# Norms of the output tiles: sums taken with the residual's addition, squares summed on ScalarE, constant and power on GpSimd

## The chip, the cores and the metric

The kernel runs on one core of a Trainium2 chip. The metric is the device time of one execution in microseconds; lower is better. The core has TensorE (PE, with its weight loads PEld), VectorE (DVE), ScalarE (ACT), GpSimd (POOL) and SyncE (SP, which issues the transfers here). Each engine works through its own queue in order; semaphores make one engine wait for another.

## The reference

Four layers over a sequence of 2048 rows of 640 numbers, all in float32: attention, Fourier mixing, attention, Fourier mixing, each on the normalized input and added to it.

```python
def _layernorm(x, axis=-1, eps=1e-5):
    m = jnp.mean(x, axis=axis, keepdims=True)
    v = jnp.var(x, axis=axis, keepdims=True)
    return (x - m) / jnp.sqrt(v + eps)
...
    def _A_ref(x, wqkv, wo):
        B, S, D = x.shape
        H = 32; Dh = D // H; W = 256
        qkv = (x @ wqkv) ...                      # 32 heads of 20
        scores = jnp.einsum("bhqd,bhkd->bhqk", q, k) * (Dh ** -0.5)
        # a query sees itself and the 255 keys before it
        ...
        return o.reshape(B, S, D) @ wo
    def _B_ref(x, dft_seq_re, dft_seq_im, dft_hid_re, dft_hid_im):
        a = jnp.einsum("bsd,ed->bse", x, dft_hid_re)
        b = jnp.einsum("bsd,ed->bse", x, dft_hid_im)
        return jnp.einsum("ts,bse->bte", dft_seq_re, a) - jnp.einsum("ts,bse->bte", dft_seq_im, b)
    x = x + _A_ref(_layernorm(x), wqkv, wo)
    x = x + _B_ref(_layernorm(x), ...)
    x = x + _A_ref(_layernorm(x), wqkv, wo)
    x = x + _B_ref(_layernorm(x), ...)
```

## The kernel before

The 2048 rows are 16 tiles (NB) of 128 rows (P), each 640 (D) columns wide. Every product is made of three matmuls: each operand is split into a high part, which is its rounded copy, and a low part, the difference, and high x high, high x low and low x high are summed (`product3`, L172). `split` makes the parts: ScalarE copies the high part (L159), VectorE or GpSimd subtracts for the low one (L165).

An attention layer ends with its output product. The product of a tile is summed in two steps: three of five chunks of the attention output are multiplied early (`partials`, added to the residual at L900, so that `y_part(t)` holds the input plus a part of the output), and the last two in `late`. There, for each tile t, 12 matmuls (two halves of 320 columns, two chunks, three matmuls) go to banks 5 and 6 in turn, and VectorE adds bank and `y_part(t)` into the new tile `xw` (L993), which is the layer's result and is stored. In the same place the next layer's norm begins: `stats` takes mean and variance of `xw` on VectorE (two statistics, L217, one aggregation, L219, the constant, L221), a further small operation gives minus the mean (L999), GpSimd raises variance plus constant to the power -1/2 (`root`, L1004), and `norm` lets ScalarE write (xw - mean) * inverse over `y_part(t)`: a small one for the bias (L957) and a large one (L954). The normalized tile is then cut into high and low parts for the Fourier layer (`split_x`: ScalarE's high part at L159, GpSimd's low part at L165). Tiles 8 and up are first added to tile t-8 in their last 256 columns by GpSimd (`sum1`, L1070), and GpSimd takes a difference for a later product (`sum3`, L1074).

The Fourier layer's first product runs along the sequence and starts while the output tiles still come. Its steps are units (`unit`, `seq`), of 9 matmuls each (L1292): a1 0 to a1 7 take tiles 0 to 7, a2 j takes tiles j and j+8. A unit is emitted behind a tile once the parts it needs have been emitted (`need`, `normed`). Each unit also cuts the sequence matrix for the next units (`cut_to`: VectorE's differences at L1198, high parts at L159, low parts at L165).

The order of work is written out by the program. `post(delay, fn)` puts a step `delay` slots later; `tick` goes on by one slot and emits the steps that are due, in the order in which they were posted. After the heads, `spend` counts 0.147 us for each matmul of a tile and 2.05 us for a unit, and ticks once for each 0.65 us (PACE). Here `root` is posted 2 slots behind its tile, `sum3` 4, `norm` and the store of the tile 5; `norm` posts the cut into parts 2 slots later for tiles below 8, and for the others `sum1` 1 and the cut 3 slots later. The last two tiles (t14, t15, called `fast`) have the root at once and are normalized by VectorE in part (`norm_last`, L969). The waits are put in by the framework wherever one engine needs what another wrote.

Of the kernel before, what the change touches and what calls it, by code (L numbers as in the profile page):

```python
# [7 lines left out]
F32 = mybir.dt.float32  # L8
# [3 lines left out]
AF = mybir.ActivationFunctionType  # L12
OP = mybir.AluOpType
# [4 lines left out]
P = 128  # L18
S = 2048
D = 640  # L20
# [5 lines left out]
NB = S // P  # L26
# [3 lines left out]
EPS = 1e-5  # L30
# [33 lines left out]
class Net:  # L64
# [883 lines left out]
    def late(self, xsrc, xdst, hook):  # L948
        nc = self.nc
        ks = range(EARLY, KC)  # L950
        w = dict(zip(ks, self.late_w))

        def scaled(t, xw, st, nm, c0, c1):
            nc.scalar.activation(self.y_part(t)[:, c0:c1], xw[:, c0:c1], AF.Identity, bias=nm[:, 1:2], scale=st[1][:, 1:2])  # L954

        def norm(t, xw, st, nm):
            nc.scalar.activation(nm[:, 1:2], nm[:, 0:1], AF.Copy, scale=st[1][:, 1:2])  # L957
            scaled(t, xw, st, nm, 0, D)
            if t < NB // 2:
                self.post(2, lambda: self.split_x(t, 0, 384))  # L960
            else:
                j = t - NB // 2
                self.post(1, lambda: self.sum1(j, nc.gpsimd))
                self.post(3, lambda: self.split_x(j, 384, 640))

        def norm_last(t, xw, st):

            xn, j = self.y_part(t), t - NB // 2
            nc.vector.tensor_scalar(out=xn[:, 384:], in0=xw[:, 384:], scalar1=st[0][:, 0:1], scalar2=st[1][:, 1:2],  # L969
                                    op0=OP.subtract, op1=OP.mult)  # L970
            self.sum1(j, nc.vector)
            self.post(1, lambda: self.split_x(j, 384, 640, nc.vector))

        def norm_rest(t, xw, st, nm):
            nc.scalar.activation(nm[:, 1:2], nm[:, 0:1], AF.Copy, scale=st[1][:, 1:2])
            scaled(t, xw, st, nm, 0, 384)

        for t in range(NB):
            sb, i = t // 4, t % 4
            y = self.y_part(t)  # L980
            xw = self.raw()
            both = [slice(hf * 320, (hf + 1) * 320) for hf in range(2)]
            if not self.after:
                ps = [self.bank("w", 320) for _ in both]
                yield from self.in_turn(ps, [self.out_terms(self.late_o[sb], w, ks, i, hf) for hf in range(2)])
                for p, cs in zip(ps, both):
                    nc.vector.tensor_tensor(out=xw[:, cs], in0=p, in1=y[:, cs], op=OP.add)
            else:
                for hf, cs in enumerate(both):
                    p = self.bank("o", 320)  # L990
                    for _ in self.product3(p, self.out_terms(self.late_o[sb], w, ks, i, hf)):
                        yield 1
                    nc.vector.tensor_tensor(out=xw[:, cs], in0=p, in1=y[:, cs], op=OP.add)  # L993
                    if hf == 0:
                        yield 1
            self.post(5, lambda t=t, xw=xw: nc.sync.dma_start(xdst[t * P:(t + 1) * P, :], xw))
            st = self.stats(xw, False)
            nm = self.ln.tile([P, 2], F32, name="nb", tag="nb")
            nc.vector.tensor_scalar_mul(nm[:, 0:1], st[0][:, 0:1], -1.0)  # L999
            self.let_go()  # L1000
            fast = t >= NB - 2

            def root(st=st):
                nc.gpsimd.tensor_tensor(out=st[1][:, 1:2], in0=st[1][:, 0:1], in1=self.half, op=OP.pow)  # L1004
            if fast:
                root()
            else:
                self.post(2, root)
            if NB // 2 - 1 <= t < NB - 1:
                self.post(4, lambda t=t: self.sum3(t - NB // 2 + 1))  # L1010
            if fast:
                d = 3 if t == NB - 2 else 0
                self.post(4 + d, lambda t=t, xw=xw, st=st: norm_last(t, xw, st))
                self.post(8 + d, lambda t=t, xw=xw, st=st, nm=nm: norm_rest(t, xw, st, nm))
            else:
                self.post(5, lambda t=t, xw=xw, st=st, nm=nm: norm(t, xw, st, nm))
            if t == NB - 2:
                u = self.last_a2 - 1
                self.post(3, lambda u=u: self.staged(u, 0, nc.vector))
                self.post(6, lambda u=u: self.staged(u, 1))  # L1020
                self.post(9, lambda u=u: self.staged(u, 2))
            hook(t)
            self.late_t = t + 1
            yield 0
# [728 lines left out]
```

## Time and profile before

| | |
|---|---|
| time, median of 3 runs | 2170.54 us (2169.17 to 2170.84) |
| profiled execution, its own time | 2169.7 us |
| its span, first to last instruction | 2168.0 us |
| granted TensorE clock | 0.998 |
| busy: TensorE, VectorE, ScalarE, GpSimd | 98%, 74%, 54%, 43% |
| the tiles' additions, L993 | 64 times, 478 ns median, 523 to 1662 us |
| the statistics of all norms, L217 | 128 times, 475 to 480 ns median by form |
| the tiles' powers, L1004 | 32 times, 552 ns median, 1007 ns at most |
| the tiles' normalization, L954 (640 columns) | 28 times, 923 ns mean |

The profiled execution is one run of the program; its time is the span plus some 1.7 us around it. A row in order of time gives start and length in us, the engine, the line, the operation, output <- inputs with their shapes, how many alike follow each other, and in brackets how long the engine stood idle before it and which instruction ended that. A row of a group gives busy time in us and the mean length of one in ns, then idle time. In the chain of waits each piece is what the next one waited for. The two attention layers have the same sequence of work; the second runs 1078 us later than the first.

### The profile page before, as it was taken

What the parts mean: (1) busy time and instruction counts of PE and PEld (TensorE: products, weight loads), DVE (VectorE), ACT (ScalarE), POOL (GpSimd) and SP (SyncE); (2) the same over time, 40 slices, a digit from 0 to 9 for tenths busy, and PEclk for the clock granted to TensorE, in tenths of its full rate; (3) what the DMA queues carried; (4) which work ended last, traced back from release to release, by engine and by line L of the source; (5) the groups of instructions that cost most, each with busy time, mean ns of one, the idle gap of its engine ahead of it and who ended that gap; (6) DMA issues with size and microseconds to landing.
All of it is one profiled execution on the core that took longest, in us unless ns stands there. A gap on an engine that the chain in (4) does not pass through costs nothing.

```text
span 2168.0 us, 49263 instructions
## 1 busy us (share of the span) xinstructions
PE 2114.2 (98%) x17893; PEld 1765.7 (81%) x17893; DVE 1613.7 (74%) x3936; ACT 1167.3 (54%) x2611; POOL 923.4 (43%) x1455
## 2 busy tenths in 40 slices
PE   7999999899999999999999999998999999999999
PEld 7987777687878888889999877776777788888899
DVE  6448888786897868787751578887778868687787
ACT  2218877766554545543431288786765545455522
POOL 2037776876423234230230477777754323242300
PEclk9999999999999999999999999999999999999999
DMA  5556666786435453657646466667864454546653
GB/s 193 164 168 194 200 196 206 221 228 195 143 123 179 133 181 127 230 197 254 213 145 185 151 202 187 208 194 230 227 185 136 124 189 137 165 152 215 224 175 125
DMA packets 221619, 395.41 MB, mean 182 GB/s; under 512 B 39360, under 2 KB 85952, under 8 KB 221376
## 3 DMA queue, kind: packets, MB, share of 16 engines
q1 hardware_dynamic: 221376, 392.26, 57.0%
q8 instruction: 141, 2.31, 0.5%
q14 instruction: 102, 0.84, 0.1%
HBM read 273.94 MB, written 117.05 MB: 180 GB/s over the span
## 4 chain that ended last, share of the span: by engine, by line
PE 84%; DVE 5%; POOL 4%; ACT 4%; DMA 2%; issue 1%; SPq 0%; ACTq 0%; DVEq 0%; POOLq 0%
PE banks L1292 29%; PE banks L172 15%; PE banks L190 14%; PE banks L636 8%; PE banks L1547 6%; PE banks L606 6%; PE banks L576 4%; POOL big L165 1%; ACT big L954 1%; PE banks L272 1%; DVE qp L165 1%; POOL ou L1222 1%; PE banks L588 1%; POOL rs L1004 1%; ACT big L159 1%
## 5 line engine op out<-in xcount | busy, mean ns | idle before, releaser
L581 DVE CUSTOM_DVE_ANT_0 banks<-banks,mask 128x384 f32<-128x384 f32 (+2 forms) x1024 | 525.4, 559 | 153.5 <-PE banks L576 116.1
L615 ACT ACTIVATE pt<-banks 128x384 f32<-128x384 f32 (+2 forms) x1024 | 430.1, 472 | 139.9 <-PE banks L576 65.8
L606 PE MATMUL banks<-qp,kp 61*128 61x384 f32 (+2 forms) x1024 | 302.7, 365 | 10.1 <-DMA qp<-mt 7.8
L621 POOL TENSOR_SCALAR_AFFINE_SELECT pt<-pt 128x256 f32<-128x256 f32 x512 | 210.1, 411 | 178.1 <-ACT pt L615 130.2
L576 PE MATMUL banks<-kp,qp 60*128 60x384 f32 (+2 forms) x1024 | 279.3, 359 | 4.8 <-DVE mc L581 4.5
L190 PE MATMUL banks<-big,wc 64*128 64x512 f32 x1920 | 272.2, 394 | 0.4 <-DVE pt L394 0.4
L606 PEld LDWEIGHTS banks<-qp,kp 61*128 61x128 f32 x1024 | 176.9, 185 | 68.1 <-issue 27.3
L636 PE MATMUL banks<-pt,vq 128*32 128x128 f32 x5760 | 214.8, 277 | 4.1 <-POOL pt L621 4.0
L190 PEld LDWEIGHTS banks<-big,wc 64*128 64x128 f32 x1920 | 182.8, 185 | 29.6 <-ACT x L500 6.7
L636 PEld LDWEIGHTS banks<-pt,vq 128*32 128x32 f32 x5760 | 143.9, 109 | 64.7 <-issue 48.0
L576 PEld LDWEIGHTS banks<-kp,qp 60*128 60x128 f32 x1024 | 163.7, 185 | 27.4 <-DVE mc L581 16.4
L1222 POOL TENSOR_TENSOR pt<-pt,pt 128x512 f32<-128x512 f32 x36 | 62.3, 1730 | 290.4 <-DMA pt<-c 206.7
L625 POOL TENSOR_SCALAR_AFFINE_SELECT pt<-pt 128x256 f32<-128x256 f32 x448 | 184.1, 411 | 0.0
L159 ACT ACTIVATE c<-pt 128x512 fp32r<-128x512 f32 x150 | 93.6, 626 | 149.3 <-POOL pt L1198 52.7
L159 ACT ACTIVATE qp<-pt 128x512 fp32r<-128x512 f32 (+1 forms) x195 | 119.8, 624 | 91.0 <-DVE pt L1223 36.3
L165 DVE TENSOR_TENSOR c<-pt,c 128x512 fp32r<-128x512 f32 x150 | 122.3, 825 | 50.6 <-ACT c L159 48.4
L165 DVE TENSOR_TENSOR qp<-pt,qp 128x512 fp32r<-128x512 f32 (+1 forms) x195 | 150.7, 786 | 12.3 <-ACT qp L159 9.6
L1292 PE MATMUL banks<-qp,big 128*128 128x512 f32 x630 | 151.1, 391 | 4.9 <-DVE qp L165 3.9
L581 DVE DVE_READ_ACCUMULATOR2_ANT mc<- 128x1 f32 x1024 | 145.2, 142 | 0.0
L1292 PEld LDWEIGHTS banks<-qp,big 128*128 128x128 f32 x630 | 117.0, 188 | 30.9 <-DVE qp L165 5.6
L1292 PE MATMUL banks<-qp,xc 128*128 128x512 f32 x480 | 117.9, 390 | 1.5 <-DVE xc L165 1.2
L1292 PEld LDWEIGHTS banks<-qp,xc 128*128 128x128 f32 x480 | 89.8, 188 | 22.0 <-DVE xc L165 2.1
(227 smaller groups left out, 4378.8 us busy)
## 6 DMA issues: line engine op xcount, KB each, us to landing
pt<-c SPq DMA_DIRECT2D x188, 512.0 KB
qk_d<-c SPq DMA_DIRECT2D x80, 512.0 KB
kp<-qk_d SPq DMA_DIRECT2D x384, 80.0 KB
qp<-qk_d SPq DMA_DIRECT2D x384, 80.0 KB
kp<-u_d SPq DMA_DIRECT2D x32, 640.0 KB
o_d<-ou SPq DMA_DIRECT2D x64, 256.0 KB
x_d<-x SPq DMA_DIRECT2D x48, 320.0 KB
v_d<-pt SPq DMA_DIRECT2D x16, 768.0 KB
```

The lines of the kernel that those rows point to most:

```text
L159: nc.scalar.activation(hi, src, AF.Copy, scale=-1.0 if neg else 1.0)
L165: (eng or nc.vector).tensor_tensor(out=lo, in0=src, in1=hi.bitcast(F32), op=OP.subtract)
L172: self.nc.tensor.matmul(p, x, y, start=n == 0, stop=n == last)
L190: self.nc.tensor.matmul(ps[a], x[r], y[r], start=half + i == 0, stop=half == 1 and i == n - 1, skip_group_check=True)
L576: nc.tensor.matmul(p, qp[quad % 2][b:b + 60, z, qb * P:(qb + 1) * P], kp[quad % 2][b:b + 60, z, k0 * P:(qb + 1) * P], start=True, stop=True)
L581: nc.vector.tensor_tensor_reduce(out=p, in0=p, in1=self.mask[:, 384 - n * P:], scale=1.0, scalar=NEG, op0=OP.add, op1=OP.max, accum_out=mc ...
L606: nc.tensor.matmul(self.banks[:, tb[e], :n * P], kp[quad % 2][b:b + 61, z, kb * P:(kb + 1) * P], qp[quad % 2][b:b + 61, z, kb * P:(kb + n) ...
L615: nc.scalar.activation(pt[quad, kb][:, 2 * z + e, :n * P], self.banks[:, tb[e], :n * P], AF.Exp, scale=SCALE)
L621: nc.gpsimd.affine_select(out=t[:, :, 0:P], in_=t[:, :, 0:P], pattern=[[0, 2], [1, P]], compare_op=OP.is_ge, fill=0.0, base=0, channel_mul ...
L625: nc.gpsimd.affine_select(out=t[:, :, 256:384], in_=t[:, :, 256:384], pattern=[[0, 2], [-1, P]], compare_op=OP.is_gt, fill=0.0, base=0, ch ...
L636: nc.tensor.matmul(p[32 * h:32 * h + 32, :], vq[:, 96 * (kb % 4) + 21 * h:96 * (kb % 4) + 21 * h + 32], t[:, h, (qb - kb) * P:(qb - kb + 1 ...
L1292: nc.tensor.matmul(self.banks[:, bk, :], p, b[q], start=start and m == 0, stop=stop and last and m == 2, skip_group_check=True)
```

## The change

For tiles 0 to 13 the norm is made in another way. VectorE's addition of bank and `y_part(t)` also sums the new tile along its row (a tensor_tensor_reduce, one sum for each half, in `sa`). Two small VectorE operations turn the two sums into minus the mean, and into minus the mean times D ** -0.5. ScalarE squares (xw * D ** -0.5 - mean * D ** -0.5) over the tile with a sum along the row, which is the variance; the squares themselves go to `y_part(t)`, which the normalization overwrites. GpSimd adds the constant and takes the power. The squares are posted 2 slots behind the tile, constant and power 4, and the normalization 6 instead of 5. The statistics, their aggregation and VectorE's addition of the constant are gone for these tiles. Tiles 14 and 15 are as before.

```diff
             both = [slice(hf * 320, (hf + 1) * 320) for hf in range(2)]
+            fast = t >= NB - 2
+            sa = None if fast else self.ln.tile([P, 3], F32, name="sa", tag="sa")
+
+            def add(p, hf, y=y, xw=xw, sa=sa):
+                cs = both[hf]
+                if sa is None:
+                    nc.vector.tensor_tensor(out=xw[:, cs], in0=p, in1=y[:, cs], op=OP.add)
+                else:
+                    nc.vector.tensor_tensor_reduce(
+                        out=xw[:, cs], in0=p, in1=y[:, cs], scale=1.0, scalar=0.0,
+                        op0=OP.add, op1=OP.add, accum_out=sa[:, hf:hf + 1])
...
-                    nc.vector.tensor_tensor(out=xw[:, cs], in0=p, in1=y[:, cs], op=OP.add)
+                    add(p, hf)
...
-            st = self.stats(xw, False)
             nm = self.ln.tile([P, 2], F32, name="nb", tag="nb")
-            nc.vector.tensor_scalar_mul(nm[:, 0:1], st[0][:, 0:1], -1.0)
+            if fast:
+                st = self.stats(xw, False)
+                nc.vector.tensor_scalar_mul(nm[:, 0:1], st[0][:, 0:1], -1.0)
+            else:
+                st = None, self.ln.tile([P, 2], F32, name="rs", tag="rs")
+                for c, f in ((0, -1.0 / D), (1, -D ** -1.5)):
+                    nc.vector.tensor_scalar(out=nm[:, c:c + 1], in0=sa[:, 0:1], scalar1=sa[:, 1:2], scalar2=f,
+                                            op0=OP.add, op1=OP.mult)
...
+            def square(xw=xw, y=y, nm=nm, sa=sa):
+                nc.scalar.activation(y, xw, AF.Square, bias=nm[:, 1:2], scale=D ** -0.5, accum_out=sa[:, 2:3])
+
+            def inverse(st=st, sa=sa, root=root):
+                nc.gpsimd.tensor_scalar_add(st[1][:, 0:1], sa[:, 2:3], EPS)
+                root()
             if fast:
                 root()
             else:
-                self.post(2, root)
+                self.post(2, square)
+                self.post(4, inverse)
...
-                self.post(5, lambda t=t, xw=xw, st=st, nm=nm: norm(t, xw, st, nm))
+                self.post(6, lambda t=t, xw=xw, st=st, nm=nm: norm(t, xw, st, nm))
```

More of the change, by code (lines that the diff above doesn't have):

```diff
@@ L985, in late @@
                 yield from self.in_turn(ps, [self.out_terms(self.late_o[sb], w, ks, i, hf) for hf in range(2)])
-                for p, cs in zip(ps, both):
-                    nc.vector.tensor_tensor(out=xw[:, cs], in0=p, in1=y[:, cs], op=OP.add)
+                for hf, p in enumerate(ps):
+                    add(p, hf)
             else:
@@ L992, in late @@
                         yield 1
-                    nc.vector.tensor_tensor(out=xw[:, cs], in0=p, in1=y[:, cs], op=OP.add)
+                    add(p, hf)
                     if hf == 0:
@@ L996, in late @@
             self.post(5, lambda t=t, xw=xw: nc.sync.dma_start(xdst[t * P:(t + 1) * P, :], xw))
-            st = self.stats(xw, False)
             nm = self.ln.tile([P, 2], F32, name="nb", tag="nb")
-            nc.vector.tensor_scalar_mul(nm[:, 0:1], st[0][:, 0:1], -1.0)
+            if fast:
[6 more added lines that the diff above has]
+                                            op0=OP.add, op1=OP.mult)
             self.let_go()
-            fast = t >= NB - 2
             def root(st=st):
                 nc.gpsimd.tensor_tensor(out=st[1][:, 1:2], in0=st[1][:, 0:1], in1=self.half, op=OP.pow)
+            def square(xw=xw, y=y, nm=nm, sa=sa):
[3 more added lines that the diff above has]
+                root()
             if fast:
```

## The prediction

> **What bounds the kernel now.** I read the page's head first, then what each engine did in the stretch that the change touches, by windows of ten microseconds, then who waited for whom there, then the chain of waits, then single rows in order of time.
>
> ```profile
> span 2168.0 us, 49263 instructions
> 525.00:535.00 10.00, 8.04 (x46) 6.89 (x47) 9.68 (x33) 5.84 (x11) 3.39 (x5) 1.00 0.90 309
> 565.00:575.00 10.00, 10.00 (x56) 8.95 (x55) 7.26 (x20) 6.49 (x14) 6.92 (x11) 1.00 0.54 174
> PE banks L172 <- DVE x L993: 2.8, 5, 0.8
> PE banks L1292 <- DVE qp L165: 1.9, 2, 1.2
> ```
>
> The output tiles t0 to t15 of the first attention are added (L993) from 523 to 584 us. The window rows give length, TensorE, weight load, VectorE, ScalarE, GpSimd, clock. In the first VectorE is full (9.68 of 10) and TensorE is not; in the later one TensorE is full, at full clock, and VectorE has room (7.26). Only where TensorE idles can the stretch get shorter. The last two rows are TensorE's waits between 518 and 665 us: 2.8 us for the banks that the additions free, and 1.9 us for a cut of weights, 1.2 of it in this stretch. So the relief of VectorE can give at most 2.8 + 1.2 = 4.0 us in this attention.
>
> The chain of waits says what paces the second half. Its rows are start, length, piece:
>
> ```profile
> 559.83 0.30 ACT nb L957
> ...
> 563.77 0.30 ACT nb L957
> 564.10 0.92 ACT big L954
> 565.02 0.52 ACT qp L159
> 565.54 0.35 ACT kp L1346
> 565.92 0.41 ACT big L159
> 566.34 0.07 issue
> 566.40 0.74 POOL big L165
> 567.14 0.51 POOL rs L1004
> 567.68 0.30 ACT nb L957
> ```
>
> This is one turn of a loop between two in-order queues. ScalarE normalizes tile T (nb, then big L954), cuts weights for a unit of the next product, and takes the high part of the normalized tile (big L159); GpSimd then takes its low part (big L165), and only behind that in its queue stands the power (rs L1004) of tile T+1, for which ScalarE's normalization of T+1 waits. A turn is 567.68 - 563.77 = 3.91 us. TensorE is tied to it:
>
> ```profile
> 569.49 0.81 DVE L165 TENSOR_TENSOR qp<-pt,qp 128x512 fp32r<-128x512 f32 x1 [0.95 <-ACT qp L159]
> 567.71 1.92 PE L172 MATMUL banks<-qp,kp 128*128 128x320 f32 x12
> ...
> 571.53 1.92 PE L172 MATMUL banks<-qp,kp 128*128 128x320 f32 x12
> ```
>
> VectorE waits 0.95 us for the cut that ScalarE put behind a normalization, and adds t12 only behind that cut, at 570.3; the first of its two additions (0.4 to 0.5 us) frees a bank for t13's matmuls, which follow at 571.53, about 0.8 us later. TensorE's own turn, a tile's 12 matmuls and a unit's 9, is 571.53 - 567.71 = 3.82 us. The loop is thus as long as TensorE's turn, with under 1 us of slack: any lengthening of it soon lengthens every tile.
>
> **VectorE's part.** One tile costs now:
>
> ```profile
> 541.89 0.88 DVE L993 TENSOR_TENSOR x<-banks,big 128x320 f32<-128x320 f32 x2
> 542.69 0.87 DVE L217 BATCH_NORM_STATS2 st<-x 128x6 f32<-128x320 f32 x2
> 543.59 0.21 DVE L219 BATCH_NORM_AGGREGATE mv<-st 128x2 f32<-128x12 f32 x1
> 543.91 0.15 DVE L221 TENSOR_SCALAR rs<-mv 128x1 f32<-128x1 f32 x1
> 543.98 0.14 DVE L999 TENSOR_SCALAR nb<-mv 128x1 f32<-128x1 f32 x1
> 544.05 0.69 DVE L805 TENSOR_TENSOR pt<-pt,vq 128x512 f32<-128x512 f32 x1
> L581 DVE CUSTOM_DVE_ANT_0 banks<-banks,mask 128x384 f32<-128x384 f32 x896 | 482.1, 584 | 118.1 <-PE banks L576 99.7 <-PE banks L606 4.7
> L581 DVE DVE_READ_ACCUMULATOR2_ANT mc<- 128x1 f32 x1024 | 145.2, 142 | 0.0
> ```
>
> From 541.89 to 544.05: 2.16 us. The change takes out both statistics, their aggregation and the addition of the constant, and turns each addition into the form that L581 already uses, an operation with a sum and a read of the sum. L581 takes 584 ns for 384 columns, so between 487 (in proportion) and 584 for the 320 here; two plain additions of 0.48 hold VectorE for 0.80 together (542.69 - 541.89), as neighbours overlap. I take 0.45 each, the reads of 142 ns between nothing and in full, and 0.25 for the two small constants (two such rows stand 0.07 apart, and a wait): 1.15 to 1.45, I take 1.2. VectorE saves about 0.95 us (0.7 to 1.0) in each of 14 tiles per attention; t14 and t15 stay as they are.
>
> The Trainium skill, "VectorE: DVE Perf Modes", Rules for kernel authors, says that chained operations are not worth fusing because the drain stays and only the count matters. By it seven instructions become six, nothing worth naming is saved, and the forecast below would be 2181. The rows speak against it: the two statistics alone hold VectorE for 0.80 us.
>
> **What this is worth up to t8.** The power of t5 now:
>
> ```profile
> 544.14 1.01 POOL L1004 TENSOR_TENSOR rs<-rs,half 128x1 f32<-128x1 f32 x1 [3.33 <-DVE nb L999]
> ```
>
> Over t0 to t4 VectorE saves 5 x 0.95 = 4.7 us. Of this 2.7 us come through to t5's constants by my estimate: no more than TensorE's waits for the additions (2.8), since the matmuls themselves remain, and the cuts of weights, whose high parts now stand behind Squares on ScalarE, come no earlier. After that the path to the normalization is longer: before, one power of 1.01 us behind the constants, now a Square, an addition and a power. That costs 1.4 us (priced below), so t5's normalization starts about 1.3 us earlier. It started behind its power at 545.2, t8's at 559.83: three turns in 14.6 us. Here the Square of the next tile falls behind the high part and beside GpSimd's low part, so a turn is 0.4 + 0.5 for constant and power, 1.2 for the normalization, 0.5 for the cut, and 0.6 and 1.1 for the parts (the rows' 0.41 and 0.74, which are for 256 columns, taken to the 384 of these tiles): 4.3 us. Three such turns, with two more cuts of 0.5 in the first, make 13.9: a lead of 1.3 + 0.7 = 2.0 at t8, or 1.0 where GpSimd is held up in two of the turns by 0.5 us as at 544.14. I take 1.5 us.
>
> **ScalarE's and GpSimd's part from t8 on.** The order of posts decides. A tile and its unit spend 12 x 0.147 + 2.05 = 3.81 us against a pace of 0.65, that is 5.87 ticks, nearly always 6 in whole slots. For tile T added in slot S: normalization now at S+6, first sum (L1070) at S+7, high and low part at S+9; T+1's Square at S+6+2 = S+8, its inverse at S+10. So ScalarE runs normalization(T), cut, Square(T+1), high part(T), and GpSimd still has low part(T) ahead of T+1's inverse. Both new steps lie inside the loop. The units keep their place: the unit behind tile T needs T-2's parts, posted 11.7 ticks earlier, with a delay that goes from 8 to 9. The store of the tile keeps its slot, and no queue of transfers is passed.
>
> ```profile
> 561.99 0.42 ACT L159 ACTIVATE big<-big 128x256 fp32r<-128x256 f32 x1 [0.39 <-POOL big L1070]
> ...
> 577.56 0.42 ACT L159 ACTIVATE big<-big 128x256 fp32r<-128x256 f32 x1 [0.32 <-POOL big L1070]
> L232 ACT ACTIVATE kp<-kp,nm 128x640 f32<-128x640 f32 x9 | 7.4, 824 | 16.1 <-POOL nm L231 16.1
> L231 POOL TENSOR_SCALAR nm<-mv 128x1 f32<-128x1 f32 x9 | 3.3, 385 | 0.0
> 567.10 0.55 POOL L1004 TENSOR_TENSOR rs<-rs,half 128x1 f32<-128x1 f32 x1
> ```
>
> *Square:* the nearest row is L232, the same 640 columns with a column as bias, 824 ns; ScalarE's operations overlap by 0.1 us, so 0.73 of its queue. No row shows a read of a sum on ScalarE; VectorE's 0.14 is the nearest, so 0.87 (0.73 to 1.2). *Constant:* L231's 385 ns and a small wait, 0.42 (0.35 to 0.9). The upper end comes from the power's own stretch: 0.55 us at 567.10, when VectorE pauses for ScalarE, 1.01 at 544.14, beside L805.
>
> The Trainium skill, "GPSIMD Engine Reference", Key points, says that GpSimd contends with VectorE's operations on two SBUF inputs. The two power rows agree. By it the constant would cost 0.9 where such an operation runs, which is my upper end.
>
> ScalarE's present waits inside the loop are filled by the Square: the first and the last of three such rows stand above (0.39 and 0.32), together 1.04; in the turns from t9 and t10 L1346 fills them already. The five turns from t8 to t13 grow by 5 x (0.42 + 0.87) - 1.04 = 5.4 us. Less the lead of 1.5, t13's normalization is 3.9 us late. From there the present chain leads to the end of the stage:
>
> ```profile
> 579.66 0.92 ACT big L954
> ...
> 590.03 20.16 PE banks L1292 x84
> ...
> 1668.42 20.16 PE banks L1292 x84
> ```
>
> These are the normalization of t13, which leads through the cut behind it and t15's addition to TensorE's long piece from 590.03. The second attention has the same piece 1078.4 us later, so twice 3.9 = 7.8 us. The profiled execution took 2169.7 us for its span of 2168.0, so it becomes 2177.5; it lies 0.8 us under the median of the runs, so the median becomes 2178.3. With the lower ends (0.35 + 0.73, lead 2.0) it is 2.4 us each, 2175.3; with the upper ones (0.9 + 1.2, lead 1.0) 8.5 each, 2187.5.
>
> **The rivals.** *Faster, the relief is kept:* the loop does not lengthen, because new steps run while ScalarE and GpSimd idle (they are busy 6.49 and 6.92 of 10), and all 4.0 us of TensorE's waits go: 2170.5 - 8 = 2162.5. For it speak VectorE's full windows; against it the turn without slack and the places of the posts. It decides where 5 turns of constant plus Square stay under 1.04 + 1.5 us, that is 0.5 us a turn, and is whole where they vanish. *No change, only the constant is in the loop:* if the Square stands behind the high part from t8 on as well, beside the low part, a turn grows by some 0.5 us, 2.5 in five, less the lead 1.0 per attention, 2172.5. This happens where two tiles are five slots apart; the present order of powers behind low parts shows six for t8 to t13. *Much slower:* GpSimd's constant contended and a dear read-out on ScalarE, the upper end above, 2187.5; against it, VectorE has pauses there. A gain from fewer VectorE instructions elsewhere is not possible, since the change touches no other stage.
>
> **How the numbers follow.** A measurement of this kernel can tell about 0.2%, 4.3 us, from no change. The lengthened loop has 0.68, all of it above 2174.9; its own range is 2175.3 to 2187.5. Something between, with the lead and the longer loop nearly equal, has 0.17 (2166.2 to 2174.9). The relief kept has 0.15 (2162 to 2166). The range from 2165 to 2187 leaves out most of the last and the dearest tail. Slower 0.68, same 0.17, faster 0.15.
>
> **What would show it.** Right: L993 in the new form at some 0.5 us, TensorE's waits for L993 up to 540 us mostly gone, turns between nb rows of t8 to t13 of about 4.7 to 5.3 us in place of 3.9, new TensorE waits there, and the long piece of 84 matmuls at some 594 us. Wrong: turns still near 3.9, or the Square seen behind the high part of the tile before, or that piece ahead of 590.

## The result and the profile after

| | before | after |
|---|---|---|
| median of 6 runs each, us | 2170.89 (2169.17 to 2172.88) | 2179.36 (2178.0 to 2181.17) |
| ratio, 95% interval | | 1.0038 (1.0027 to 1.0049) |
| span of the profiled execution, us | 2168.0 | 2176.3 |
| granted TensorE clock | 0.998 | 0.995 |

The changed kernel is slower by 8.5 us. The windows of ten microseconds of the kernel after, at the two places shown of before, have the same columns: length, TensorE, weight load, VectorE, ScalarE, GpSimd, granted clock, DMA share, GB/s. Below them are two rows of the list of TensorE's waits between 518 and 670 us.

```profile
525.00:535.00 10.00, 8.45 (x51) 7.42 (x49) 6.96 (x29) 8.31 (x18) 4.58 (x8) 1.00 0.85 285
...
565.00:575.00 10.00, 8.54 (x46) 7.06 (x45) 3.93 (x14) 7.04 (x16) 5.75 (x11) 1.00 0.56 181
```

```profile
PE banks L172 <- DVE sa L991: 4.1, 6, 1.0
PE banks L1317 <- DVE qp L165: 2.3, 3, 1.5
```

The busy engine has changed. VectorE falls from 9.68 to 6.96 of 10 in the first window and from 7.26 to 3.93 in the later one; its work is gone as meant. But in the later window TensorE, full before, idles 1.46 of 10 us: it waits for the additions (L991) again, now for another reason, which stands in VectorE's own row of each turn (VectorE's rows in order of time, then TensorE's; the bracket is the wait ahead of a row):

```profile
566.53 0.81 DVE L165 TENSOR_TENSOR qp<-pt,qp 128x512 fp32r<-128x512 f32 x1 [2.58 <-ACT qp L159]
...
571.59 0.81 DVE L165 TENSOR_TENSOR qp<-pt,qp 128x512 fp32r<-128x512 f32 x1 [3.06 <-ACT qp L159]
```

```profile
567.80 2.02 PE L172 MATMUL banks<-qp,kp 128*128 128x320 f32 x12 [0.49 <-DVE sa L991]
...
572.87 2.02 PE L172 MATMUL banks<-qp,kp 128*128 128x320 f32 x12 [0.98 <-DVE sa L991]
```

VectorE stands 2.6 to 3.1 us for a cut of weights that ScalarE makes behind a normalization, where it stood 0.95; the additions queue behind that cut, and TensorE behind the additions. The chain of waits (start, length, piece) shows why the normalization is late. This is one turn, from nb to nb:

```profile
564.72 0.31 ACT nb L957
565.05 0.92 ACT big L954
565.98 0.52 ACT qp L159
566.50 0.48 ACT kp L1371
566.98 0.81 ACT big L1024 x2
567.79 0.32 ACT big L159
568.17 0.74 POOL big L165
568.91 0.19 POOL rs L1027
569.18 0.58 POOL rs L1021
569.78 0.30 ACT nb L957
```

Set beside the turn of before, two pieces are new: the Square with its read of the sum (L1024, 0.81 us) ahead of the high part, and the constant (L1027, 0.27 us from its start to the power's) behind the low part. The turn is 569.78 - 564.72 = 5.06 us where it was 3.9.

I call a stage what lies between the first matmuls of `late` on weights (the first row of 18 matmuls of L172; 521.97 us before, 521.22 after) and the long piece of TensorE that the prediction followed. The table gives for each kernel, in the first and the second attention, when t8 is normalized after the start of the stage, how long it is from there to t13's normalization, and the length of the stage; all are differences between starts of rows.

| kernel | median us | ratio to before (95%) | t8 at, us | t8 to t13, us | stage, us |
|---|---|---|---|---|---|
| before | 2170.89 | | 37.86, 37.86 | 19.50, 19.51 | 68.06, 68.07 |
| after | 2179.36 | 1.0038 (1.0027 to 1.0049) | 38.92, 38.17 | 23.86, 23.85 | 73.47, 72.71 |
| first8 | 2165.68 | 0.9978 (0.9969 to 0.9986) | 35.53, 35.54 | 20.08, 20.08 | 66.30, 66.64 |
| last6 | 2177.38 | 1.0034 (1.0021 to 1.0046) | 37.40, 37.52 | 23.85, 23.85 | 71.94, 72.07 |
| vector_alone | 2159.64 | 0.9952 (0.9939 to 0.9964) | 33.19, 33.19 | 19.54, 19.53 | 63.43, 63.41 |
| scalar_alone | 2185.39 | 1.0069 (1.0055 to 1.0083) | 41.01, 42.17 | 23.86, 23.86 | 75.56, 76.73 |
| square_later | 2179.39 | 1.0046 (1.0033 to 1.0058) | 40.33, 40.33 | 21.70, 21.70 | 72.73, 72.73 |
| square_later_from8 | 2175.31 | 1.0020 (1.0012 to 1.0029) | 38.94, 39.84 | 21.73, 21.72 | 71.36, 72.30 |
| before_root_ahead | 2165.81 | 0.9981 (0.9972 to 0.9990) | 36.39, 36.37 | 17.95, 17.51 | 65.79, 65.78 |
| inverse_ahead | 2163.84 | 0.9969 (0.9958 to 0.9980) | 34.47, 34.46 | 18.48, 18.49 | 65.74, 65.74 |
| inverse_ahead_norm5 | 2164.56 | 0.9971 (0.9959 to 0.9982) | 37.12, 37.13 | 18.36, 18.36 | 66.18, 66.19 |
| inverse_ahead_norm5_from8 | 2160.32 | 0.9952 (0.9938 to 0.9965) | 34.47, 34.46 | 18.49, 18.48 | 64.49, 64.48 |
| first8_ahead | 2162.55 | 0.9964 (0.9951 to 0.9976) | 34.06, 34.07 | 18.99, 18.94 | 64.51, 64.80 |
| t1_to_t7_ahead | 2162.55 | 0.9959 (0.9945 to 0.9973) | 33.87, 33.87 | 18.96, 18.93 | 64.29, 64.61 |

Each ratio is against runs of the kernel before on the same chip; its medians there were 2169.8 to 2171.0. Outside the stages one profiled execution differs from another: from the end of the first stage to the start of the second it took 1010.3 us before, 1009.3 after, and 1008.4 to 1011.3 in the others. So the two stages of the changed kernel are 10.0 us longer together while its median is 8.5 higher; the profiled execution is 1.0 us shorter between the stages and starts the first stage 0.75 us sooner. Whether the change has any part in that difference is open.

### The profile page after: what moved, and what is told of

Same layout as the page of the kernel before. It is cut to its first block, busy times and chain, and to the rows that moved or that the text cites. A ratio compares the mean times of both kernels' runs of the same rounds, so it can differ in the third digit from the quotient of the medians.

```text
span 2176.3 us, 49321 instructions
## 1 busy us (share of the span) xinstructions
PE 2120.7 (97%) x17893; PEld 1767.8 (81%) x17893; DVE 1580.1 (73%) x3908; ACT 1189.6 (55%) x2667; POOL 930.8 (43%) x1483
## 4 chain that ended last, share of the span: by engine, by line
PE 83%; DVE 5%; ACT 5%; POOL 4%; issue 1%; DMA 1%; SPq 0%; POOLq 0%; ACTq 0%; DVEq 0%
PE banks L1317 28%; PE banks L172 15%; PE banks L190 14%; PE banks L636 8%; PE banks L1572 6%; PE banks L606 6%; PE banks L576 4%; POOL big L165 1%; ACT big L954 1%; PE banks L272 1%; ACT big L1024 1%; POOL ou L1247 1%; DVE qp L165 1%; POOL rs L1021 1%; PE banks L588 1%
## 5 line engine op out<-in xcount | busy, mean ns | idle before, releaser
L165 DVE TENSOR_TENSOR qp<-pt,qp 128x512 fp32r<-128x512 f32 (+1 forms) x195 | 149.1, 777 | 25.6 <-ACT qp L159 22.8
L165 DVE TENSOR_TENSOR c<-pt,c 128x512 fp32r<-128x512 f32 x150 | 122.4, 825 | 57.6 <-ACT c L159 55.2
L1317 PE MATMUL banks<-qp,big 128*128 128x512 f32 x630 | 155.5, 398 | 7.0 <-DVE qp L165 4.2
```

The source lines that it names most:

```text
L165: (eng or nc.vector).tensor_tensor(out=lo, in0=src, in1=hi.bitcast(F32), op=OP.subtract)
L1317: nc.tensor.matmul(self.banks[:, bk, :], p, b[q], start=start and m == 0, stop=stop and last and m == 2, skip_group_check=True)
```

## The experiments

My theory after the result: the cost is what stands inside the loop between ScalarE's and GpSimd's queues, and the loop exists because the constant and the power of tile T+1 stand behind the low part of T. The rival: ScalarE and GpSimd simply have more to do, and the place makes no difference.

**Parts of the change alone.** The first two kernels give the new norm to half of the tiles each:

```diff
+            old = fast or t >= NB // 2      # first8;  last6: old = fast or t < NB // 2
...
-            if fast:
+            if old:
                 st = self.stats(xw, False)
...
+            elif old:
+                self.post(2, root)
...
-                self.post(6, lambda t=t, xw=xw, st=st, nm=nm: norm(t, xw, st, nm))
+                self.post(5 if old else 6, lambda t=t, xw=xw, st=st, nm=nm: norm(t, xw, st, nm))
```

> The new norm for t0 to t7 only, the old one for t8 to t13. My theory: the loss is made where GpSimd's low part of tile T stands ahead of tile T+1's inverse, t8 to t13, where five turns grew by 4.36 us per attention; up to t8 the changed kernel was only 1.06 and 0.31 us late. So this comes out at 2171 to 2173, turns between normalizations of t8 to t13 back at 3.9 us. Rival: the loss is made early, by the Squares that delay the cuts of weights on ScalarE among t0 to t5 and by TensorE's slower clock after its pause there. Then this stays at 2177 to 2180.

> The old norm for t0 to t7, the new one for t8 to t13. My theory: five turns longer by about 0.87 us each, 4.4 per attention, 2170.9 + 8.7 = 2179.6, with the stretch up to t8 as in the kernel before. Rival (the loss is made early): 2171 to 2173.

last6 carries the cost: t8 to t13 takes 23.85 us, as in the changed kernel and 4.35 more than before, and the time is 6.9 us above the runs of before beside it (2170.44); that is 2.2 us less than expected, in part because t8 comes 0.5 and 0.3 us earlier than before. first8 is faster than before by 4.8 us (3.2 of it within the two stages), which I had not expected. The reason lies in one turn. GpSimd's rows in first8, in order of time:

```profile
554.20 1.11 POOL L165 TENSOR_TENSOR big<-big,big 128x384 fp32r<-128x384 f32 x1 [2.30 <-ACT big L159]
555.28 0.22 POOL L1028 TENSOR_SCALAR rs<-sa 128x1 f32<-128x1 f32 x1
555.59 0.57 POOL L1022 TENSOR_TENSOR rs<-rs,half 128x1 f32<-128x1 f32 x1
556.12 0.74 POOL L1102 TENSOR_TENSOR kp<-big 128x256 f32<-128x256 f32 x1
556.82 1.00 POOL L1022 TENSOR_TENSOR rs<-rs,half 128x1 f32<-128x1 f32 x1
558.45 1.12 POOL L165 TENSOR_TENSOR big<-big,big 128x384 fp32r<-128x384 f32 x1 [0.64 <-ACT big L159]
```

The power at 555.59 is t7's, behind a low part. t8 has the old norm, its power (556.82) is posted two slots behind the tile and stands ahead of t7's low part (558.45). t8's normalization follows t7's after 2.09 us; the same turn is 4.78 before and 4.97 after. Against the turn of before, this one exchange of neighbours in a queue was worth some 2.7 us, which pointed to the order.

The next two take the parts of the change by kind of engine. vector_alone keeps VectorE's new additions and leaves Square and constant away: it computes no variance, takes the power of the larger of the row's sum and 1, and so does not give the layer's result; its power and normalization stand in the slots of before. scalar_alone keeps Square, constant and power and gives VectorE its statistics and plain additions back.

```diff
# vector_alone
-                for c, f in ((0, -1.0 / D), (1, -D ** -1.5)):
+                for out, f, op in ((nm[:, 0:1], -1.0 / D, OP.mult), (st[1][:, 0:1], 1.0, OP.max)):
...
-                self.post(2, square)
-                self.post(4, inverse)
+                self.post(2, root)
...
-                self.post(6, lambda t=t, xw=xw, st=st, nm=nm: norm(t, xw, st, nm))
+                self.post(5, lambda t=t, xw=xw, st=st, nm=nm: norm(t, xw, st, nm))
# scalar_alone
-                if sa is None:
+                if True:                     # plain addition
...
+                st = self.stats(xw, False)
...
```

> VectorE's part alone: additions with sums, two small operations, then the power at its old slot; the squares and the constant are left out, the power is taken of the larger of the row's sum and 1, so the norm's scale is another. My theory: nothing lengthens the loop, VectorE's relief comes through in part: up to 4.0 us per attention by TensorE's waits, some 3, so 2163 to 2166. Rival (up to t8 the path over ScalarE and GpSimd is as long as VectorE's, the relief is worth nothing): 2170 to 2171.

> ScalarE's and GpSimd's part alone: plain additions, statistics and aggregation stay on VectorE and give the mean; the variance comes from Square, constant and power as in the change (VectorE's own constant is computed too and not used). My theory: the loop is as long as in the change and no relief stands against it: 4.4 per attention from t8 on and 1.5 to 2.5 before it, 2183 to 2185. Rival (the added steps cost only through their share of busy time on engines that are not full): 2171 to 2173.

VectorE's relief by itself is worth 10.8 us, more than I had expected; the added steps by themselves cost 14.95. The two do not add up: their sum is 4.2 us slower, and the whole change is 8.5 slower. Beside the added steps the relief is worth only 6.0 us (2185.39 to 2179.36): t8 comes 2.1 and 4.0 us earlier by it in the two attentions, 4.7 in vector_alone. The window that holds the second part of the stage, vector_alone first, then scalar_alone:

```profile
555.00:600.00 45.00, 43.55 (x216) 36.34 (x214) 32.47 (x89) 26.97 (x56) 20.18 (x28) 1.00 0.37 122
```

```profile
555.00:600.00 45.00, 38.69 (x184) 30.56 (x183) 31.11 (x88) 27.70 (x59) 23.98 (x38) 0.96 0.31 106
```

scalar_alone's TensorE is idle 6.3 of 45 us, vector_alone's 1.45. Yet in scalar_alone neither ScalarE (27.70 of 45) nor GpSimd (23.98) is near full: it isn't the amount of their work that holds TensorE, which speaks against the rival.

**The place of the Square.** In the changed kernel the Square was posted three slots behind the tile, first for all tiles, then from t8 on:

```diff
-                self.post(2, square)
+                self.post(3, square)                            # square_later
+                self.post(3 if t >= NB // 2 else 2, square)     # square_later_from8
```

> The changed kernel with its Square posted three slots behind the tile instead of two; from t8 on it then stands behind the high part on ScalarE, beside GpSimd's low part, and the constant and the power stay behind that low part. My theory (the cost from t8 on is what stands inside the loop of ScalarE and GpSimd): the Square, 0.81 us, leaves the loop, the constant (0.2 to 0.3) stays, turns from t8 to t13 of about 4.2 to 4.4 us instead of 4.8, some 2.3 us less in each attention: about 2174.8. Rival (the place makes no difference, ScalarE and GpSimd simply have more to do): 2179, turns still 4.6 to 5.1.

> The changed kernel with its Square posted three slots behind the tile for t8 to t13 alone, two for t0 to t7. With three everywhere the turns from t8 fell to 4.33 us as expected, but t8's normalization came 1.4 to 2.2 us later, and the time stayed at 2179.4. My theory: the place of the Square inside the loop does cost its amount, and only the first eight tiles ate it up; here t8 starts as in the changed kernel (38.2 to 38.9 us after the start of the stage), five turns of 4.33 follow, and the end comes 1.8 to 2.2 us earlier in each attention: about 2175.3 (2174.5 to 2176.5). Rival (the Square's place makes no difference to the end): 2178.5 to 2179.5.

In square_later the Square does move behind the high part, as ScalarE's rows show, and the turns from t8 fall to 4.33:

```profile
569.00 0.41 ACT L159 ACTIVATE big<-big 128x256 fp32r<-128x256 f32 x1
569.31 0.82 ACT L1024 ACTIVATE big<-x,nb 128x640 f32<-128x640 f32 x1
```

```profile
536.53 0.49 PE L1317 MATMUL banks<-qp,big 128*128 128x512 f32 x1 [1.83 <-ACT qp L159]
```

But the time stayed, and the theory's 2174.8 was missed. The last row, TensorE's, tells where part of it went: at the first unit TensorE waits 1.83 us for a cut, 1.09 in the changed kernel. t5 is normalized 0.7 and 1.5 us later in the two attentions, and the turn behind it takes 6.58 us in place of 5.90; so t8 comes 1.4 to 2.2 us later, which eats up the gain. With the later place from t8 on alone the time is 2175.31, where 2175.3 was expected. The place of the Square matters, by 2.1 us in five turns. That the time met the forecast so closely is partly luck: in the profiled execution the second stage is only 0.4 us shorter, because t8 comes 1.7 us later there, behind a fall of the granted clock to 0.50 from 1618 us.

**The order of GpSimd's queue.** inverse_ahead is the changed kernel with both new steps posted one slot behind the tile. before_root_ahead does the same with the power of the kernel before.

```diff
# inverse_ahead                      # before_root_ahead
-    self.post(2, square)            -    self.post(2, root)
-    self.post(4, inverse)           +    self.post(1, root)
+    self.post(1, square)
+    self.post(1, inverse)
```

> The changed kernel with the Square and with constant and power both posted one slot behind the tile, the normalization six as before. From t8 on GpSimd's queue then holds constant and power of tile T+1 ahead of the low part of T, and ScalarE's the Square ahead of the high part. My theory: normalization of T+1 no longer waits for the low part of T, so the loop between the two queues is broken, turns fall to TensorE's 3.8 to 3.9 us, and VectorE's relief stays: 2161 to 2166. Rival (the added Square, constant and power cost by their amount, wherever they stand): turns stay over 4.4 us and the time at 2175 or above.

> The kernel before with its power posted one slot behind the tile instead of two, so that it stands ahead of the low part of the tile before on GpSimd. It tells how much of a gain of the changed kernel with the same order would be the order's alone. My theory: the loop of before (3.87 us) was hardly longer than TensorE's turn (3.82), so little is won: 2168 to 2170.5. Rival (the order of GpSimd's queue was already the bound before): 5 us or more faster, 2160 to 2166.

GpSimd's rows of inverse_ahead, and a window of the same kernel:

```profile
563.22 0.22 POOL L1027 TENSOR_SCALAR rs<-sa 128x1 f32<-128x1 f32 x1 [0.47 <-ACT big L1024]
563.53 0.57 POOL L1021 TENSOR_TENSOR rs<-rs,half 128x1 f32<-128x1 f32 x1
564.06 0.74 POOL L165 TENSOR_TENSOR big<-big,big 128x256 fp32r<-128x256 f32 x1
```

```profile
565.00:575.00 10.00, 10.00 (x55) 8.88 (x54) 5.95 (x19) 8.47 (x18) 7.27 (x14) 1.00 0.47 176
```

Constant and power stand ahead of the low part. In this window TensorE is full and ScalarE is at 8.47 of 10, with every Square, constant and power still done; in the changed kernel TensorE was at 8.54 there and ScalarE at 7.04. The same instructions are some 15 us faster (2163.84 against 2179.36), 14.7 of it within the two stages. The rival, by which added work costs wherever it stands, is out.

before_root_ahead went against my theory of "little": it is 4.0 us faster than before, and its time lies in the rival's range, though the rival's gain of 5 us or more was not reached. The kernel before was itself held by the loop. This does not show where I looked, in the windows from 555 to 585 in which TensorE is full, but mostly behind them. First TensorE's rows of the kernel before at the end of the stage; then the windows there of before and of before_root_ahead:

```profile
586.11 0.73 PE L1292 MATMUL banks<-qp,big 128*128 128x512 f32 x2 [0.70 <-DVE qp L165]
587.35 1.65 PE L1292 MATMUL banks<-qp,big 128*128 128x512 f32 x6 [0.50 <-ACT big L159]
590.03 0.97 PE L1292 MATMUL banks<-c,rr 128*128 128x512 f32 x3 [1.03 <-ACT rr L159]
```

```profile
585.00:595.00 10.00, 7.77 (x32) 5.32 (x31) 8.51 (x22) 6.95 (x17) 0.98 (x1) 1.00 0.46 142
```

```profile
585.00:595.00 10.00, 9.40 (x42) 7.36 (x40) 8.57 (x21) 8.13 (x19) 0.00 (x0) 1.00 0.45 140
```

The three waits make 2.23 us; in before_root_ahead one of 0.60 is left. That is 1.6 of the 2.27 us by which its stage is shorter. Of the rest 0.1 is in the earlier waits, and 0.6 in TensorE's busy time, which falls from 61.6 to 61.1 us for the same 327 matmuls. Most of the loop's lateness had been paid at the end.

**Which tiles, and the end of the stage.** first8_ahead has the new norm in t0 to t7 (Square, constant and power one slot behind) and the old one, its power one slot behind, in t8 to t13; t1_to_t7_ahead has the old norm in t0 too. In both the old norm keeps its normalization five slots behind. inverse_ahead_norm5 posts the normalization of inverse_ahead five slots behind instead of six, inverse_ahead_norm5_from8 does so from t8 on alone.

```diff
+            old = fast or t >= NB // 2                # first8_ahead
+            old = fast or t == 0 or t >= NB // 2      # t1_to_t7_ahead
...
-                self.post(6, lambda t=t, xw=xw, st=st, nm=nm: norm(t, xw, st, nm))
+                self.post(5, ...)                            # inverse_ahead_norm5
+                self.post(6 if t < NB // 2 else 5, ...)      # inverse_ahead_norm5_from8
```

> The new norm for tiles 0 to 7 with Square, constant and power posted one slot behind the tile, and the old norm for tiles 8 to 13 with the power posted one slot behind. My theory: VectorE's relief is taken where VectorE is full (t0 to t7), nothing is added where TensorE is full, and no power waits behind a low part: 2160 to 2165, as fast as the changed kernel with the inverse ahead or up to 3 us faster. Rival (the gain of the new norm in the first eight tiles alone came from the one broken turn between t7 and t8): no better than that kernel's 2165.7, up to 2169.

> The kernel with the new norm for the first eight tiles and all powers one slot behind, with the old norm for tile 0 as well, so the new one for t1 to t7. In the kernel with t0 included TensorE waits 1.56 us for the second tile's bank, because VectorE stands 0.94 us behind a cut of weights that ScalarE makes only behind t0's Square. My theory: without that Square the cut comes about 1.6 us earlier, the wait falls to about 0.5, and what remains of it reaches the end of the stage: 0.5 to 1.1 us in each attention, 2160.3 to 2161.6. Rival (the cuts behind the later Squares, where TensorE waits 0.61 twice, set the stage anyway): 2162.5, or 0.5 to 1 more because VectorE has t0's statistics again.

> The changed kernel with Square, constant and power posted one slot behind the tile, and the normalization five slots behind, as in the kernel before, instead of six. In the kernel with six the power of t14 stands on GpSimd ahead of t13's sum, and t15's addition waits behind the cut that follows it: TensorE's long piece starts 65.7 us after the start of the stage, as in the kernel before with its power ahead, though t14 was added 1.3 us earlier. My theory: with five slots t13's sum goes first and the 1.2 us of each attention come through: 2161 to 2162. Rival (ScalarE's Squares in the second half hold the cuts of weights, wherever the normalization stands): 2163.8 or more.

> The changed kernel with Square, constant and power posted one slot behind the tile, and the normalization five slots behind for t8 to t13 alone, six for t0 to t7. With five everywhere the turns from t5 to t7 were 6.6 and 4.75 us again, with the power behind the low part, and the time was 2164.6; so the test of the end was spoilt by the beginning. My theory: t5 to t8 now as with six everywhere (t8's normalization 34.5 us after the start of the stage), and at the end t13's sum stands ahead of t14's power on GpSimd, so TensorE's long piece starts some 64.5 us after the start in place of 65.7: 2161 to 2162. Rival (what ScalarE has more to do from t8 on holds the end, wherever the normalization stands): 65.7 again, 2163.8.

first8_ahead is at 2162.55 us, inside the theory's range, and the rival's 2165.7 or more is out.

t1_to_t7_ahead: the wait of 1.56 us did go, but two of 0.55 and 0.57 came in its place, since VectorE has t0's statistics again; the stage is 0.2 us shorter and the time the same. My expectation failed there.

inverse_ahead_norm5 missed its forecast of 2161 to 2162; its median is 0.7 us above that of inverse_ahead, and the intervals of the two ratios overlap. Its turns from t5 to t7 are 6.59 and 4.75 us, where inverse_ahead has 5.11 and 3.57, with a low part in front of the power again; this is its chain:

```profile
547.34 1.91 POOL big L165
...
549.52 1.07 POOL rs L1021
```

In these tiles the low part comes two slots behind the normalization. At five that is slot seven, which with tiles six slots apart is the slot of the next tile's power as well, and the low part was posted earlier. From t8 on the parts come three slots behind. With five from t8 on alone the beginning is that of inverse_ahead (t8 at 34.47), and what I had read out of the end of inverse_ahead could be tested: there the power of t14 (first row, GpSimd) stood ahead of t13's sum, and in inverse_ahead_norm5_from8 (last two rows) it stands behind it.

```profile
578.46 0.99 POOL L1021 TENSOR_TENSOR rs<-rs,half 128x1 f32<-128x1 f32 x1 [1.50 <-DVE nb L1012]
579.42 0.82 POOL L1095 TENSOR_TENSOR big<-big,big 128x256 f32<-128x256 f32 x1
```

```profile
575.88 0.74 POOL L1095 TENSOR_TENSOR big<-big,big 128x256 f32<-128x256 f32 x1
577.43 0.99 POOL L1021 TENSOR_TENSOR rs<-rs,half 128x1 f32<-128x1 f32 x1 [0.80 <-DVE nb L1012]
```

The stage falls from 65.74 to 64.49 us, 64.5 expected, and the time to 2160.32, a little below what was expected. This kernel, the whole change in another order, beats both kernels: 0.9952 of before (0.9938 to 0.9965).

How much of this belongs to the order and how much to the new norm stays open. before_root_ahead, the old norm with its power ahead, is at 0.9981, 5 to 6 us slower. But its slots are those of inverse_ahead_norm5, and there the new norm is at 0.9971, with overlapping intervals and a stage 0.4 us longer (66.18 against 65.79). At equal slots a gain from the new norm is not shown. The later normalization of t0 to t7, which brought the new norm from 2164.56 to 2160.32, was not tried with the old one.

## Why the prediction was right, and which terms were not

The forecast was 2178.3 us and the median 2179.36. The mechanism was the one forecast, a longer loop from t8 on that outweighs VectorE's relief. Two terms of the sum were off, in opposite directions, and that they partly cancel is luck.

*VectorE's tile, 1.2 us.* Right. A tile whose parts follow each other without a pause in the kernel after, additions, reads, two constants, and the next operation:

```profile
549.58 0.48 DVE L991 CUSTOM_DVE_ANT_0 x<-banks,big 128x320 f32<-128x320 f32 x1
549.99 0.08 DVE L991 DVE_READ_ACCUMULATOR2_ANT sa<- 128x1 f32 x1
549.99 0.48 DVE L991 CUSTOM_DVE_ANT_0 x<-banks,big 128x320 f32<-128x320 f32 x1
550.40 0.08 DVE L991 DVE_READ_ACCUMULATOR2_ANT sa<- 128x1 f32 x1
550.51 0.34 DVE L1016 TENSOR_SCALAR nb<-sa 128x1 f32<-128x1 f32 x2
550.77 0.68 DVE L1223 TENSOR_TENSOR pt<-pt 128x512 f32<-128x512 f32 x1
```

550.77 - 549.58 = 1.19 us, against 2.16. The Trainium skill's rule ("VectorE: DVE Perf Modes", Rules for kernel authors) that fusing chained operations does not pay is not borne out here: six instructions take VectorE 1.19 us where seven took 2.16. vector_alone, which has the fused form and computes no variance, is 10.8 us faster.

*The relief can give at most 4.0 us in an attention.* Wrong: vector_alone's stage is 4.63 us shorter. The step that failed is the premise that only TensorE's idle time can shrink, and that only two kinds of it would. The waits for the additions fall from 2.8 to 0.9 us and that for the first unit's cut from 1.2 to 0.7, which is 2.4 of the 4.0. Behind 585 us, which I left out, 2.23 us fall to 1.45, as these rows of vector_alone's TensorE show:

```profile
583.98 1.65 PE L1316 MATMUL banks<-qp,big 128*128 128x512 f32 x6 [0.42 <-ACT big L159]
586.66 0.99 PE L1316 MATMUL banks<-c,rr 128*128 128x512 f32 x3 [1.03 <-ACT rr L159]
```

Most of what is left, 1.25 us, is TensorE's busy time, 61.6 us before and 60.4 here for the same 327 matmuls. In part it goes with the number of waits: in the kernel before, twelve matmuls of L172 take 2.02 us right behind a wait (at 552.31) and 1.92 without one. The rest of it is open.

*t5's constants 2.7 us earlier.* By the chain they are ready at 542.28, 21.06 us into the stage, against 544.13 - 521.97 = 22.16 before: 1.1 us earlier in the first attention and 1.8 in the second. The cut of weights holds it, as these rows of VectorE and TensorE show:

```profile
534.79 1.08 DVE L165 TENSOR_TENSOR qp<-s,qp 128x512 fp32r<-128x512 f32 x1 [1.62 <-ACT qp L159]
```

```profile
534.81 0.49 PE L1317 MATMUL banks<-qp,big 128*128 128x512 f32 x1 [1.09 <-ACT qp L159]
535.93 3.30 PE L1317 MATMUL banks<-qp,big 128*128 128x512 f32 x8 [0.62 <-DVE qp L165]
```

The prediction had let the cuts come no earlier. In fact ScalarE, full of Squares there (8.31 of 10), took VectorE's place as the bound.

*The lead of 1.5 us at t8.* The mis-sized term. The path from t5's constants to its normalization grew by 1.2 us, near the 1.4 priced. But the three turns to t8, put at 13.9 us, took 15.61, and 14.65 before. The chain has the pieces: GpSimd's low part 1.28 us and the constant 0.63 in the first of these turns, the power 1.07 in the second, where I had put 1.1, 0.4 and 0.5. That is 1.0 of the 1.7 us. The rest is an order that I had wrong: in the third turn, from t7 to t8, the Square already stands ahead of the high part, where it was to stand behind it, and adds its 0.81 us. ScalarE's rows:

```profile
556.85 0.82 ACT L1024 ACTIVATE big<-x,nb 128x640 f32<-128x640 f32 x1
...
557.67 0.51 ACT L159 ACTIVATE big<-big 128x384 fp32r<-128x384 f32 x1
```

So t8 was 1.06 us late in the first attention and 0.31 in the second, outside even the lead of 1.0 to 2.0 from which the range was made.

*Five turns grow by 5.4 us.* They grew by 4.36. The Square takes 0.81 us instead of 0.87, the constant 0.27 instead of 0.42, and 5 x (0.81 + 0.27) - 1.04 = 4.36: the form of the sum holds, its prices were high. That it meets the hundredth is chance: single turns grew by 0.64 to 1.16 us, up to 0.1 off what the sum gives for them. Turns of 4.57 to 5.07 stand against 4.7 to 5.3 forecast. One reading behind the upper price was wrong: at 567.10 VectorE did not pause but ran statistics (L217, 0.87 us), and the power beside them took 0.55 us all the same.

*From t13's normalization to the end nothing changes.* Right for this kernel: 10.70 us before and 10.69 after (with the inverse ahead it is 12.79). Together 5.4 and 4.6 us in the two attentions where 3.9 was forecast for each; the median came nearer than that, 8.5 against 7.8, because of the difference outside the stages, and that is luck too.

*The order of the queues* from t8 on was as derived: Square ahead of the high part, constant and power behind the low part. The rival that left only the constant in the loop is what square_later_from8 does from t8 on; its turns grew by 0.45, forecast 0.5. The rival that keeps the relief, put at 2162.5, came true when the order was changed: 2163.8 in inverse_ahead, and 2160.3 with the normalization moved as well.

## What to carry to other kernels

Price a new step by its place in the in-order queues, before its duration: the same change cost 8.5 us with constant and power behind a neighbour's low part and saved 6.0 with them ahead of it, 10.7 with the normalization's slot set as well. When TensorE is full in a window, look on to where the chain ends before calling the chain harmless; lateness is carried forward and paid at the next join. And after moving a step, see what it now shares a slot with in each part of the loop: the normalization's slot that was right from t8 on was wrong before.

## What the runs showed of the hardware that I had not expected

The granted clock fell to half for 3 to 4 us. The kernel after, first the stretch from 537 us (TensorE idled 1.09 and 0.62 us just ahead of it), then TensorE at the same place in the second attention:

```profile
537.00:538.00 1.00, 1.00 (x4) 0.81 (x3) 1.00 (x2) 0.97 (x2) 1.00 (x2) 0.50 0.06 23
```

```profile
1618.69 2.12 PE L1317 MATMUL banks<-qp,big 128*128 128x512 f32 x8 [0.62 <-DVE qp L165]
```

The clock is the 0.50 in the first row. Eight matmuls took 3.30 us, against 2.12 in the second attention after the same two waits: this is the difference of 0.74 us between the two attentions at t5. The same two waits of 1.7 us together, 0.5 us apart, are thus followed by a fall in one attention and by none in the other. No such fall shows in either stage of before, vector_alone, before_root_ahead or of any kernel with the inverse ahead, though inverse_ahead has a single wait of 1.56 us, and before has the three of 0.70, 0.50 and 1.03 within 5 us. What brings a fall about is not shown. A like fall at the end of the stage, from 591 us, was hidden: t13's normalization to the long piece took 10.69 us with it and 10.70 in the kernel before, without. The Trainium skill, "TensorE: Matmul & The Clock Gate", Why this matters for your kernels, puts the limit at an idle gap of about 3 us. These falls do not agree with it: in the changed kernel no wait just ahead of one is longer than 1.5 us.

Reading the sum on ScalarE is cheap: its row is 0.19 us long, and Square and read hold the queue for 0.81. The constant on GpSimd takes 0.36 us in the mean of 28. In eight of them, in which VectorE ran 512-column operations of L165 or L1223 for most of the time, it takes 0.66 to 0.75; beside the additions from banks (L991), the small operations or nothing it takes 0.21 to 0.23.
